# Banded attention and two MLPs on one core: an RMS norm's sums with tokens on partitions, its roots spread through device memory

## Chip, cores and metric

The kernel runs on 1 core of one Trainium2 chip. The metric is device time in microseconds (us). Before the change it is 637.46 us, the median of 3 runs (635.98 to 637.98). The engines of the core are named as in the profile: PE (TensorE), DVE (VectorE), ACT (ScalarE), POOL (GpSimd) and SP (SyncE, which here only issues transfers).

## The reference

For 2 x 768 tokens: banded attention with 8 heads of 64, then a first MLP with a squared ReLU (d_model 512, d_ff 2048), then a second, gated MLP (d_ff 1536) with an RMS norm ahead of it. The change is in that norm.

```python
x = attention(q, k, v)                       # 1536 x 512
h = np.maximum(x @ w_in, 0.0)
x = h * h @ w_out                            # first MLP
rms = np.sqrt(np.mean(x * x, axis=-1, keepdims=True) + 1e-06)
xn = x / rms * rms_g
g = xn @ w_gate
silu = g * (1.0 / (1.0 + np.exp(-g)))
out = silu * (xn @ w_val) @ w_out2           # second MLP
```

## The kernel before

The activations of both MLPs lie with the model dimension on partitions and the tokens along the free dimension: `x` and `y` are 4 blocks (e = 0..3) of 128 features. Tokens are worked in 4 chunks (c = 0..3) of 384 (`CH`). Two chunks make a half (p = 0: chunks 0 and 1; p = 1: chunks 2 and 3). Every value that goes into a product is kept as a high and a low part, and a product is three matmuls (`mm3`, lines 385 to 387). Products of a half are formed from seven block products in place of eight (`quad`), on sums and differences of the two chunks' blocks, which `norm` also prepares (lines 637, 642, 375, 376). The tiles `ar` and `x` hold the results.

The order in time around the change: attention (to about 140 us) with the first part of the first MLP between it, the rest of the first MLP, and from about 290 us its last group of hidden features, chunk by chunk (`first`), where line 517 adds the last part to `y`. When a chunk's `y` is whole, `norm_sum(c, bank)` makes its vector of 1/rms: ACT squares the four blocks (lines 602, 607), DVE adds the squares (line 608), one PE matmul with a 128x128 matrix of ones (line 610) sums over the 128 partitions and at the same time puts each token's sum on all 128 partitions, ACT takes the root on 128x384 (line 613), and DVE the reciprocal in three pieces of 128x128 (line 616). The result stands in the tile `ns` of the chunk (two tiles, c % 2). `norm(p)` then multiplies y, g and ns (line 637) and makes the operands of the gate and value products of the half. The gated MLP works over 6 pairs of hidden blocks and 2 halves; its first pair, first half, needs only chunks 0 and 1, its first pair, second half, needs chunks 2 and 3.

Weights come through SP (line 415) into two raw tiles `wraw`, and are expanded by ACT (lines 416, 418), DVE (line 420) and a split (lines 375, 376). A transfer of a weight block is issued when its raw tile is free. Queues work in order on every engine: an instruction that waits holds those behind it.

The order of all instructions is not written by hand. Each operation is added to a plan with its engine, an assumed duration, the tiles it reads and writes and, for PE, a due time; `Plan.solve` places all of them by due time, backward and forward in several rounds, takes the order with the earliest planned end, and `emit` issues the instructions in that order. Where the plan leaves PE free in two set stretches of time, it puts filler matmuls (line 1362) there. The plan takes a transfer as landed 2.6 us after its own duration (`LAT["SP"]`).

Of the kernel before, what the change touches and what calls it, by code (L numbers as in the profile page):

```python
# [12 lines left out]
F32 = mybir.dt.float32  # L13
# [6 lines left out]
P = 128  # L20
# [4 lines left out]
DM = 512  # L25
KD = DM // P
CH = 384
# [49 lines left out]
class Plan:  # L77
# [6 lines left out]
    def __init__(self):  # L84
        self.ops, self.ahead = [], set()
        self.wrote, self.read = {}, {}
# [182 lines left out]
class Mlp:  # L269
# [5 lines left out]

    def __init__(self, nc, plan, tl, main, late, psm, psl, srcs, gcol, epst, ones, ident, out):
        self.nc, self.plan, self.tl, self.out = nc, plan, tl, out
        self.gcol, self.epst, self.ones, self.ident, self.srcs = gcol, epst, ones, ident, srcs  # L280
        for k in range(KD):
            for h in "hl":
                tl.define(f"x{h}{k}", main, [P, NTOK], F32R)
        for p in range(2):
            tl.define(f"y{p}", main, [P, KD * 2 * CH], F32)
        for n in range(NM + 1):
            tl.define(f"M{n}", main if n < NM else late, [P, 1024], F32R)
        for n in range(HB):
            tl.define(f"h{n}", main, [P, 2 * CH], F32R)
        for n in range(2):  # L290
            tl.define(f"wraw{n}", main, [P, 1026], I32)
            tl.define(f"p5{n}", late, [P, CH], F32)
            tl.define(f"ns{n}", late, [P, CH], F32)
        for n in range(3):
            tl.define(f"wbits{n}", main, [P, 512], F32)
            tl.define(f"H{n}", late, [P, 512], F32R)
        for n in range(5):
            tl.define(f"ra{n}", main if n < 3 else late, [P, CH], F32)
        for n in range(4):
            tl.define(f"nq{n}", late, [P, CH], F32)  # L300
        tl.define("ar", late, [P, 24 * CH], F32R)
        for n in range(8):
            tl.define(f"b{n}", psm if n < 4 else psl, [P, 512], F32)
        self.nraw = self.nbits = self.nload = self.nact = self.nra = self.np5 = self.nnq = 0
        self.nhalf = 0
        self.clock = 0.0
        self.late = ["late"]
        self.attention_over = False
        self.w = {}
# [229 lines left out]
            self.relu2(lambda f=f: self.tl(f"b{banks[f]}")[:, :CH], [("b", banks[f])], act[f, c % 2])  # L539
        return act  # L540

    def outs(self, f0, cs, act):
        nc = self.nc
        for c in cs:
            for e in range(KD):
                bank = e % 2
                ps = lambda bank=bank: self.tl(f"b{bank}")[:, :CH]
                y, ry = (lambda e=e, c=c: self.y(e, c)), self.yres(e, c)
                for f in range(2):
                    w, rw = self.w[("out", f0 + f), e]  # L550
                    self.mm3(bank, w, act[f, c % 2][0], f == 0, f == 1, CH, rw + self.both(act[f, c % 2][1]))
                self.op("DVE", DVE(CH), lambda y=y, ps=ps: nc.vector.tensor_tensor(  # L552
                    out=y(), in0=ps(), in1=y(), op=ALU.add), [("b", bank)] + ry, ry)
                yield
# [41 lines left out]
    def norm_sum(self, c, bank):  # L596
# [3 lines left out]
        for e in range(KD):  # L600
# [5 lines left out]
            t, rt = (lambda n=n: tl(f"nq{n}")), [("nq", n)]  # L606
            self.op("ACT", ACT(CH), lambda e=e, t=t: nc.scalar.activation(t(), self.y(e, c), AF.Square), self.yres(e, c), rt)
            self.op("DVE", DVE(CH), lambda t=t: nc.vector.tensor_tensor(out=s(), in0=s(), in1=t(), op=ALU.add), rs + rt, rs, port=True)
        ps = lambda: tl(f"b{bank}")[:, :CH]
        self.op("PE", 0.75, lambda: nc.tensor.matmul(  # L610
            ps(), lhsT=self.ones, rhs=s(), start=True, stop=True, skip_group_check=True), rs, [("b", bank)],
            due=self.clock - (12.0 if bank == 7 else 0.0), mode="full", slack=NSLACK)
        self.op("ACT", ACT(CH) + 1.3, lambda: nc.scalar.activation(
            s(), ps(), AF.Sqrt, bias=self.epst, scale=1.0 / DM), [("b", bank)], rs)
        for i in range(NT):
            self.op("DVE", 0.85, lambda i=i: nc.vector.reciprocal(  # L616
                s()[:, i * P : (i + 1) * P], s()[:, i * P : (i + 1) * P]), rs, rs)

    def norm(self, p):

# [681 lines left out]
def kernel(  # L1302
# [23 lines left out]
    with ExitStack() as cx:  # L1326
        cx.enter_context(tc.manual_schedule(engines=None))
        plan, tl = Plan(), Lazy()
        main, psm = Late(tc, cx, "main"), Late(tc, cx, "psm", **space)
        late, psl = Late(tc, cx, "late"), Late(tc, cx, "psl", **space)  # L1330
        main(), psm()
        ax = ExitStack()
        ap, psa = Late(tc, ax, "attn"), Late(tc, ax, "psa", **space)
        ap(), psa()
        mlp = Mlp(nc, plan, tl, main, late, psm, psl, srcs, gcol, epst, ones, ident, out)
        fetch, count, nl, ng = scalars(nc, const, counts)
        att = Attention(nc, plan, tl, ap, psa, mlp, kq, vab, ident, nl, ng)
        plan.add("ACT", 0.45, fetch, (), ["nw"], due=0.0, lat=LAT["SP"])
# [26 lines left out]
    with tc.If(said["value"] < 1):  # L1365
        with ExitStack() as cx:
            plan, tl = Plan(), Lazy()
            main, psm = Late(tc, cx, "gmain"), Late(tc, cx, "gpsm", **space)
            main()
            late = Late(tc, cx, "glate")  # L1370
            mlp = Mlp(nc, plan, tl, main, late, psm, psm, srcs, gcol, epst, ones, ident, out)
            general_attention(tc, kq, vab, nl, ng, ident, mlp)
            for c in range(NC_ - 1):
                mlp.begin(c, None)
            mlp.rest(mlp.clock)
            plan.solve().emit()
# [62 lines left out]
```

## Time and profile before

| | |
|---|---|
| median of 3 runs | 637.46 us |
| profiled execution | 636.76 us, of which the span of instructions is 635.0 us |
| PE busy | 624.0 us (98% of the span) |
| DVE busy | 454.4 us (72%) |
| ACT busy | 421.7 us (66%) |
| POOL busy | 158.9 us (25%) |
| chain that ended last | PE 88%, DVE 4%, ACT 4%, DMA 2%, issue 1%, POOL 1% |
| PE clock granted | 0.999 of full speed |

Times of instructions are from the profiled execution and count from the first instruction of the span. A busy PE is one with a matmul in it: matmuls overlap, so one of 384 columns is listed with some 0.34 us while the next starts 0.17 us later; the spacing of the starts shows what one costs. Fill matmuls count as busy, too. "Idle before" an instruction is its engine's idle time, and the arrow says whose end it waited for.

### The profile page before, as it was taken

How to read it: one execution, taken by the hardware profiler on the slowest of the kernel's cores; microseconds unless marked ns; L12 is line 12 of the kernel's file. 1: busy time of each engine (PE TensorE's matmuls, PEld its weight loads, DVE VectorE, ACT ScalarE, POOL GpSimd, SP SyncE). 2: the span in 40 equal slices, each digit the busy share in tenths (PEclk: the TensorE clock that was granted, in tenths of full speed). 3: DMA queues.
4: the chain of work that ended last, by engine and by line, in shares of the span. 5: the costliest groups of instructions: out<-in, count | busy, mean ns of one | idle time of the engine just before them, and what ended most of it. 6: DMA issues, size and time to landing. Idle time of an engine off the chain costs nothing.

```text
span 635.0 us, 10497 instructions
## 1 busy us (share of the span) xinstructions
PE 624.0 (98%) x3740; PEld 591.7 (93%) x3740; DVE 454.4 (72%) x1007; ACT 421.7 (66%) x954; POOL 158.9 (25%) x235
## 2 busy tenths in 40 slices
PE   8899999999999999999999999999999999999996
PEld 8789899999999999999999989999999998999995
DVE  6777989859998777785569998458458458546444
ACT  5899797958977887775659877846445445453310
POOL 6442455332404300042001204221232133140000
PEclk9999999999999999999999999999999999999999
DMA  7875767101224244233000111423213114010023
GB/s 238 231 233 156 202 163 192 42 12 66 67 67 129 71 133 133 66 105 97 0 1 1 67 35 34 132 67 100 67 35 123 43 34 133 33 35 2 0 91 114
DMA packets 20845, 56.34 MB, mean 89 GB/s; under 512 B 3248, under 2 KB 6064, under 8 KB 20784
## 3 DMA queue, kind: packets, MB, share of 16 engines
q1 hardware_dynamic: 19472, 53.82, 27.9%
q10 hardware_dynamic: 1312, 1.77, 0.8%
q8 instruction: 31, 0.51, 0.3%
q14 instruction: 30, 0.25, 0.1%
HBM read 52.43 MB, written 3.15 MB: 88 GB/s over the span
## 4 chain that ended last, share of the span: by engine, by line
PE 88%; DVE 4%; ACT 4%; DMA 2%; issue 1%; POOL 1%; POOLq 0%; ACTq 0%; DVEq 0%
PE b L386 26%; PE b L385 26%; PE b L387 26%; PE tb L1065 2%; PE av L1075 2%; PE ps L1026 2%; PE b L1362 1%; DMA wraw<-in_w_in_dram 1%; ACT p L1048 1%; PE ps L1034 1%; DVE p L1044 1%; DMA wraw<-in_w_out_dram 1%; DVE ns L616 0%; DVE wbits L420 0%; DVE qs L983 0%
## 5 line engine op out<-in xcount | busy, mean ns | idle before, releaser
L385 PE MATMUL b<-xh,M 128*128 128x384 f32 x384 | 132.3, 345 | 0.2 <-ACT ra L481 0.2
L387 PE MATMUL b<-xh,M 128*128 128x384 f32 x384 | 129.1, 336 | 0.0
L386 PE MATMUL b<-xl,M 128*128 128x384 f32 x384 | 129.1, 336 | 0.0
L376 POOL TENSOR_TENSOR M<-wbits,M 128x512 fp32r<-128x512 f32 x32 | 47.2, 1480 | 158.2 <-ACT M L375 158.1
L385 PEld LDWEIGHTS b<-xh,M 128*128 128x128 f32 x384 | 72.2, 188 | 2.5 <-ACT ra L481 0.6
L386 PEld LDWEIGHTS b<-xl,M 128*128 128x128 f32 x384 | 72.1, 188 | 2.1 <-DVE xl L376 0.3
L387 PEld LDWEIGHTS b<-xh,M 128*128 128x128 f32 x384 | 72.1, 188 | 0.2
L385 PE MATMUL b<-h,M 128*128 128x384 f32 x208 | 71.7, 345 | 0.0
L386 PE MATMUL b<-h,M 128*128 128x384 f32 x208 | 70.0, 337 | 0.1
L387 PE MATMUL b<-h,M 128*128 128x384 f32 x208 | 69.7, 335 | 0.0
L742 DVE TENSOR_TENSOR y<-b,y 128x512 f32<-128x512 f32 (+1 forms) x61 | 41.6, 682 | 37.2 <-PE b L387 36.2
L375 ACT CAST M<-wbits 128x512 fp32r<-128x512 f32 x81 | 49.9, 621 | 19.5 <-PE b L387 9.9
L420 DVE SCALAR_TENSOR_TENSOR wbits<-wraw,wbits 128x512 int32<-128x512 int32 x68 | 47.3, 695 | 16.4 <-ACT wbits L418 12.6
L456 POOL TENSOR_TENSOR wbits<-wbits 128x256 f32<-128x256 f32 x16 | 13.3, 833 | 174.9 <-DVE wbits L420 174.9
L386 PE MATMUL b<-M,h 128*128 128x512 f32 (+1 forms) x146 | 56.9, 390 | 0.0
L385 PE MATMUL b<-M,h 128*128 128x512 f32 (+1 forms) x146 | 56.8, 389 | 0.0
L387 PE MATMUL b<-M,h 128*128 128x512 f32 (+1 forms) x146 | 56.8, 389 | 0.0
L1048 ACT ACTIVATE p<-p,few 128x256 f32<-128x256 f32 (+1 forms) x96 | 46.9, 497 | 12.5 <-DVE few L1044 8.7
L416 ACT ACTIVATE wbits<-wraw 128x512 f16<-128x512 bf16 x68 | 45.2, 668 | 11.9 <-POOL wbits L456 5.8
L484 DVE TENSOR_TENSOR h<-ra,h 128x384 fp32r<-128x384 f32 x64 | 39.3, 618 | 13.0 <-ACT ra L483 12.6
L552 DVE TENSOR_TENSOR y<-b,y 128x384 f32<-128x384 f32 x64 | 34.6, 551 | 13.5 <-PE b L387 13.5
L709 ACT ACTIVATE ra<-b 128x384 f32<-128x384 f32 x36 | 17.6, 491 | 39.9 <-PE b L387 39.9
(145 smaller groups left out, 1540.7 us busy)
## 6 DMA issues: line engine op xcount, KB each, us to landing
wraw<-in_w_out_dram SPq DMA_DIRECT2D x28, 512.0 KB, 3.4
wraw<-in_w_in_dram SPq DMA_DIRECT2D x16, 512.0 KB, 4.1
wraw<-in_w_gate_dram SPq DMA_DIRECT2D x12, 512.0 KB, 3.3
wraw<-in_w_val_dram SPq DMA_DIRECT2D x12, 512.0 KB, 3.3
raw<-in_kq_dram SPq DMA_DIRECT2D x16, 240.0 KB, 4.7
raw<-in_kq_dram SPq DMA_DIRECT2D x16, 208.0 KB, 4.8
v<-in_vab_dram SPq DMA_DIRECT2D x8, 384.0 KB, 3.1
v<-in_vab_dram SPq DMA_DIRECT2D x8, 256.0 KB, 3.5
```

The source lines that it names most:

```text
L375: self.op("ACT", ACT(n), lambda: nc.scalar.copy(dst()[0], src()), rs, [(x, "hi") for x in ws])
L376: self.op(eng, t(n), lambda: e.tensor_tensor(out=dst()[1], in0=src(), in1=f32(dst()[0]), op=ALU.subtract), rs + [(x, "hi") for x in ws], [ ...
L385: nc.tensor.matmul(ps, lhsT=wh, rhs=ah, start=first, stop=False, skip_group_check=True)
L386: nc.tensor.matmul(ps, lhsT=wh, rhs=al, start=False, stop=False, skip_group_check=True)
L387: nc.tensor.matmul(ps, lhsT=wl, rhs=ah, start=False, stop=last, skip_group_check=True)
L416: self.plan.add("ACT", ACT(512), lambda: nc.scalar.activation(tl(bits)[:, 256:].bitcast(F16), head(), AF.Copy), rr, rb)
L420: self.plan.add("DVE", DVE(512), lambda: nc.vector.scalar_tensor_tensor(out=bi(), in0=tail(), scalar=13, in1=bi(), op0=ALU.logical_shift_r ...
L484: self.op("DVE", DVE(CH), lambda: nc.vector.tensor_tensor(out=get()[1], in0=t(), in1=f32(get()[0]), op=ALU.subtract), rt + hi, lo, port=True)
L552: self.op("DVE", DVE(CH), lambda y=y, ps=ps: nc.vector.tensor_tensor(out=y(), in0=ps(), in1=y(), op=ALU.add), [("b", bank)] + ry, ry)
L709: self.op("ACT", ACT(CH), lambda: nc.scalar.activation(t(), src(), AF.Silu), rs, rt)
L742: self.op("DVE", DVE(a1 - a0), lambda o=o, ps=ps: nc.vector.tensor_tensor(out=o(), in0=ps(), in1=o(), op=ALU.add), [("b", bank)] + ro, ro)
L1048: self.op("ACT", 0.29 + w / 1200, lambda j=j: nc.scalar.activation(tl(f"p{m}")[:, j, :w], tl(f"p{m}")[:, j, :w], AF.Exp, bias=tl("few")[:, ...
```

## The change

The sum over the features is taken with the roles of the two matmul operands exchanged. In place of one matmul with the ones as the stationary operand and 384 tokens moving, there are three, each with 128 tokens of `ns` as the stationary operand (every third token: column i, i + 3, ...) and one column of ones moving. Their results stand in a 128x3 piece of PSUM: token 3p + i on partition p, column i. ACT's root and DVE's reciprocal work on this 128x3 (a new tile `rt`). SP then stores it to a new tile `far` in device memory, where the 384 values lie in the order of the tokens, and loads it from there to all 128 partitions of `ns`. From there on all is as before: `ns` holds 1/rms for each of the 384 tokens on every partition.

The function `outs` gets an argument `on` (empty unless given) with which ACT would carry the running `y` through PSUM. No call gives it.

```diff
-        ps = lambda: tl(f"b{bank}")[:, :CH]
-        self.op("PE", 0.75, lambda: nc.tensor.matmul(
-            ps(), lhsT=self.ones, rhs=s(), start=True, stop=True, skip_group_check=True), rs, [("b", bank)],
-            due=self.clock - (12.0 if bank == 7 else 0.0), mode="full", slack=NSLACK)
-        self.op("ACT", ACT(CH) + 1.3, lambda: nc.scalar.activation(
-            s(), ps(), AF.Sqrt, bias=self.epst, scale=1.0 / DM), [("b", bank)], rs)
-        for i in range(NT):
-            self.op("DVE", 0.85, lambda i=i: nc.vector.reciprocal(
-                s()[:, i * P : (i + 1) * P], s()[:, i * P : (i + 1) * P]), rs, rs)
+        ps, r, rr = (lambda: tl(f"b{bank}")[:, :NT]), (lambda: tl(f"rt{c % 2}")), [("rt", c % 2)]
+        far, rf = (lambda: tl(f"far{c}")), [("far", c)]
+
+        def sums():
+            for i in range(NT):
+                nc.tensor.matmul(ps()[:, i : i + 1], lhsT=s().rearrange("p (n i) -> p i n", i=NT)[:, i], rhs=self.ones[:, :1],
+                                 start=True, stop=True, skip_group_check=True)
+        self.op("PE", 0.25 * NT, sums, rs, [("b", bank)], due=self.clock - (12.0 if bank == 7 else 0.0), mode="full", slack=NSLACK)
+        self.op("ACT", ACT(NT) + 1.4, lambda: nc.scalar.activation(
+            r(), ps(), AF.Sqrt, bias=self.epst, scale=1.0 / DM), [("b", bank)], rr)
+        self.op("DVE", 0.16, lambda: nc.vector.reciprocal(r(), r()), rr, rr)
+        self.op("SP", 0.1, lambda: nc.sync.dma_start(
+            out=far().rearrange("a (p i) -> (a p) i", i=NT), in_=r()), rr, rf)
+        self.op("SP", DMA(192), lambda: nc.sync.dma_start(out=s(), in_=far().broadcast_to([P, CH])), rf, rs)
...
+            tl.define(f"rt{n}", late, [P, NT], F32)
...
+        for n in range(NC_):
+            tl.define(f"far{n}", far, [1, CH], F32)
...
+        far = Late(tc, cx, "far", space=bass.MemoryType.DRAM)
```

## Rows read from the trace of the kernel before

**Rows 1.** The page's part 1: busy time, share of the span, instructions.
```profile
PE 624.0 (98%) x3740; PEld 591.7 (93%) x3740; DVE 454.4 (72%) x1007; ACT 421.7 (66%) x954; POOL 158.9 (25%) x235
```

**Rows 2.** Table by stretches: stretch, length, busy time per engine, clock, DMA share, GB/s.
```profile
290.00:345.00 55.00, 55.00 (x315) 54.47 (x314) 36.82 (x68) 34.67 (x71) 1.61 (x1) 1.00 0.06 20
345.00:366.00 21.00, 20.92 (x118) 20.06 (x116) 19.42 (x33) 17.84 (x33) 4.53 (x5) 1.00 0.15 51
```

**Rows 3.** PE's timeline: start, duration, instruction, idle time before it and its releaser.
```profile
365.41 0.34 PE L386 MATMUL b<-xl,M 128*128 128x384 f32 x1
365.58 0.34 PE L387 MATMUL b<-xh,M 128*128 128x384 f32 x1
366.33 0.94 PE L1362 MATMUL b<-ones 128*128 128x128 f32 x6 [0.41 <-DVE ra L713]
367.02 0.43 PE L385 MATMUL b<-ar,H 128*128 128x384 f32 x1
...
376.98 0.34 PE L385 MATMUL b<-xh,M 128*128 128x384 f32 x1
```

**Rows 4.** PE's groups of instructions from 345 to 372 us: count, busy us, mean ns.
```profile
L1362 PE MATMUL b<-ones 128*128 128x128 f32 x10 | 1.7, 284 | 0.4 <-DVE ra L713 0.4
```

**Rows 5.** Chain of waits that ended last: start, us, engine, tile, line, count.
```profile
33.05 1.24 PE av L1075 x20
...
348.48 0.65 PE b L610 x2
```

**Rows 6.** DVE's timeline, columns as in Rows 3.
```profile
355.61 0.94 DVE L616 RECIPROCAL ns<-ns 128x128 f32<-128x128 f32 x1
356.47 0.49 DVE L608 TENSOR_TENSOR ns<-ns,nq 128x384 f32<-128x384 f32 x1
...
363.72 0.94 DVE L616 RECIPROCAL ns<-ns 128x128 f32<-128x128 f32 x1
365.12 0.69 DVE L420 SCALAR_TENSOR_TENSOR wbits<-wraw,wbits 128x512 int32<-128x512 int32 x1 [0.45 <-issue]
365.72 0.55 DVE L713 TENSOR_TENSOR ra<-b,ra 128x384 f32<-128x384 f32 x1
...
366.66 0.61 DVE L637 SCALAR_TENSOR_TENSOR nq<-y,gcol,ns 128x384 f32<-128x384 f32 x1
```

**Rows 7.** ACT's timeline, columns as in Rows 3.
```profile
359.23 1.28 ACT L613 ACT_TABLE_LOAD   x1
360.52 0.58 ACT L613 ACTIVATE ns<-b,epst 128x384 f32<-128x384 f32 x1
...
364.39 0.63 ACT L418 ACTIVATE wbits<-wbits 128x512 int32<-128x512 int16 x1
```

**Rows 8.** Tile ns: duration ns least/median/most, first and last start, shapes.
```profile
L616 DVE RECIPROCAL ns<-ns x12: 893/941/952, 309.1 to 363.7; 128x128 f32<-128x128 f32 x12
L610 PEld LDWEIGHTS b<-ns,ones x8: 187/188/188, 305.8 to 358.3; 128*128 128x128 f32 x8
```

**Rows 9.** Small instructions of other lines (1055 and 1146), columns as in Rows 8.
```profile
L1055 DVE RECIPROCAL few<-few x48: 151/164/167, 10.8 to 133.0; 128x2 f32<-128x2 f32 x48
...
L1146 ACT ACTIVATE warm<-epst x1: 204/204/204, 3.7 to 3.7; 128x1 f32<-128x1 f32 x1
```

**Rows 10.** DMA issues: tile, queue, count, KB each, us from issue to landing.
```profile
v<-in_vab_dram SPq DMA_DIRECT2D x8, 64.0 KB, 3.6
out_dram<-y SPq DMA_DIRECT2D x6, 256.0 KB, 2.0
...
gcol<-in_rms_g_dram SPq DMA_DIRECT2D x1, 2.0 KB, 4.7
```

**Rows 11.** SP's timeline from 290 to 385 us: start and duration of the issue.
```profile
348.69 0.33 SPq L415 DMA_DIRECT2D wraw<-in_w_gate_dram  x1
358.73 0.33 SPq L415 DMA_DIRECT2D wraw<-in_w_val_dram  x1
365.83 0.33 SPq L415 DMA_DIRECT2D wraw<-in_w_out_dram  x1
```

More of the change, by code (lines that the diff above doesn't have):

```diff
@@ L269, with __init__ @@
 class Mlp:
-    def __init__(self, nc, plan, tl, main, late, psm, psl, srcs, gcol, epst, ones, ident, out):
+    def __init__(self, nc, plan, tl, main, late, far, psm, psl, srcs, gcol, epst, ones, ident, out):
         self.nc, self.plan, self.tl, self.out = nc, plan, tl, out
@@ L540, in plain, with outs @@
         return act
-    def outs(self, f0, cs, act):
+    def outs(self, f0, cs, act, on=()):
         nc = self.nc
@@ L548, in outs @@
                 y, ry = (lambda e=e, c=c: self.y(e, c)), self.yres(e, c)
+                if e in on:
+                    self.op("ACT", ACT(CH), lambda y=y, ps=ps: nc.scalar.copy(ps(), y()), ry, [("b", bank)])
                 for f in range(2):
                     w, rw = self.w[("out", f0 + f), e]
-                    self.mm3(bank, w, act[f, c % 2][0], f == 0, f == 1, CH, rw + self.both(act[f, c % 2][1]))
+                    self.mm3(bank, w, act[f, c % 2][0], f == 0 and e not in on, f == 1, CH, rw + self.both(act[f, c % 2][1]))
+                if e in on:
+                    self.op("ACT", ACT(CH), lambda y=y, ps=ps: nc.scalar.copy(y(), ps()), [("b", bank)], ry)
+                    yield
+                    continue
                 self.op("DVE", DVE(CH), lambda y=y, ps=ps: nc.vector.tensor_tensor(
@@ L1334 @@
         ap(), psa()
-        mlp = Mlp(nc, plan, tl, main, late, psm, psl, srcs, gcol, epst, ones, ident, out)
+        mlp = Mlp(nc, plan, tl, main, late, far, psm, psl, srcs, gcol, epst, ones, ident, out)
         fetch, count, nl, ng = scalars(nc, const, counts)
@@ L1370 @@
             late = Late(tc, cx, "glate")
-            mlp = Mlp(nc, plan, tl, main, late, psm, psm, srcs, gcol, epst, ones, ident, out)
+            far = Late(tc, cx, "gfar", space=bass.MemoryType.DRAM)
+            mlp = Mlp(nc, plan, tl, main, late, far, psm, psm, srcs, gcol, epst, ones, ident, out)
             general_attention(tc, kq, vab, nl, ng, ident, mlp)
```

## The prediction

> **What bounds the kernel now.** I read the busy shares first: TensorE (PE) works for 624.0 of 635.0 us [rows 1]. A change on another engine is therefore worth only what it gives back of the PE's remaining time, or what it adds by stopping it. The change touches the stretch from 290 to 385 us, so the table by stretches came next. From 290 to 345 us PE is busy 55.00 of 55.00 us, DVE only 36.82; from 345 to 366 us PE has 20.92 of 21.00, but DVE 19.42 and ACT 17.84 [rows 2]. The norms of chunks 0 and 1 lie in the first stretch, beside a PE that waits for nobody; those of chunks 2 and 3 lie where DVE and ACT are nearly full.
>
> Then PE's own timeline, since a busy PE can hide filler. Two kinds of loss stand in it.
>
> The sums themselves: in the chain of waits the two records of chunk 2's matmul with ones stand with 0.65 us [rows 5], so the four norm sums cost PE 2.6 us.
>
> The stall: product matmuls start 0.17 us apart (365.41, 365.58), but behind the one at 365.58 the next PE instruction starts at 366.33, 0.75 us later, and it is filler (L1362) that computes nothing the output needs. Three fills (six matmuls) last from 366.33 to 367.02, 0.23 us each; there are five (ten matmuls) from 345 to 372. So at most 0.58 + 5 x 0.23 = 1.73 us is lost here. The idle time ahead of the filler ends with DVE's L713 [rows 3, 4].
>
> Why L713 is late needs two timelines. On DVE the last reciprocal of chunk 3 runs from 363.72 to 364.66, then DVE stands idle 0.45 us, then L420 (365.12), then L713 (365.72) [rows 6]. On ACT the L418 that L420 needs starts at 364.39 and ends at 365.02; before it stand a table load of 1.28 us (359.23), the root (360.52, 0.58) and what follows [rows 7]. So both engines are late at once: the reciprocals hold DVE until 364.66, ACT holds it 0.45 us longer.
>
> **The change, part by part.**
>
> *Reciprocals.* Out go 12 of 941 ns, median [rows 8]; in come 4 on 128x3. The nearest row is a reciprocal on 128x2: 164 ns [rows 9]. DVE gains 12 x 0.94 - 4 x 0.16 = 10.6 us, half of it (5.3 us) for chunks 2 and 3, in the stretch where DVE is full. On PE that is worth nothing by itself; it is worth the stall as far as DVE causes it.
>
> *Roots.* ACT's root on 128x384 takes 0.58 us [rows 7]; an activation on 128x1 took 0.204 us [rows 9]. ACT gains some 0.38 us per norm. The table loads stay: between 0 and no gain, I count none. The 0.38 us together with an earlier start can pull L418 forward by about as much as DVE stood idle for it.
>
> *Matmuls.* Two matmuls of 384 columns (fp32 is recorded as two) become three products, so six records, each with its own 128x128 weight load and one column moving. No row shows this. Below: 20 small ones with weights of 64 columns (av) take 1.24 us, 0.062 each, so 6 x 0.062 = 0.37 us [rows 5]. Above: the record of a 128x128 load is 188 ns [rows 8]; if nothing overlaps, and the stride of three words costs nothing more, 6 x 0.188 = 1.13 us. The nearest are the fills: 128x128 fp32 weights, 0.69 us for six [rows 3]. I take 0.69 against 0.65, +0.04 each, so +0.2 us for four, with ends at 4 x (0.37 - 0.65) = -1.1 and 4 x (1.13 - 0.65) = +1.9 us.
>
> *The two transfers.* After the reciprocal SP stores 1.5 KB to device memory, waits for it to land, and issues a load of it to all 128 partitions (192 KB). Stores of 256 KB land 2.0 us after issue; the load of g, made of 4-byte pieces like the new 12-byte ones, took 4.7; loads of 64 KB took 3.6 [rows 10]. For the store I take 2.0 (same direction, same queue), with 4.7 as the upper end; for the load 3.6, with 4.7 above and the store's 2.0 below.
>
> The Trainium skill (DMA: Bandwidth & Descriptors, Anatomy of one DMA) gives about 2.0 us of fixed cost plus bytes over 436 GB/s, measured on another issuing path; for 192 KB that is an estimate of 2.45 us. The row of 64 KB disagrees: 3.6 us. By the page the pair would take 4.5 us and the vector would come 1.1 us earlier than below.
>
> *The vector's date.* For chunk 3 today: root starts at 360.52, the vector is whole at 364.66, 4.1 us [rows 6, 7]. After: 0.20 + 0.16 + 2.0 + 3.6, plus three hand-overs that I put at 0.1 each, 6.3 us. The start moves the other way: the third sum (L608, 356.47) had to wait until chunk 2's reciprocal of 355.61 was over (0.94 us); without it that sum runs 0.86 us earlier [rows 6]. So the vector lands at about 360.52 - 0.86 + 6.3 = 366.0 instead of 364.66. Its first reader, L637, ran at 366.66 today because DVE had other work first [rows 6]. That work, with 5.3 us taken off DVE, is the cover: the reader is not late, and the work before it (L713 among it) moves forward. What is late next after L713 is ACT's L418.
>
> For chunks 0 and 1 the vector comes some 2 us later than now. The cover is PE's chunk-3 work, which needs no norm, and DVE's 18 idle us of 55 [rows 2]. I count nothing; without that cover each late us before gate products of the first half is one us of PE.
>
> *SP's queue.* A wait there holds every transfer behind it: first for the reciprocal, then for the landing of the store. Weight loads are issued at 348.69, 358.73 and 365.83 [rows 11]. Chunk 2's pair would be issued from about 350 to 352.5 and chunk 3's from 360 to 362.5, both between these. I count nothing. A load that falls behind a pair is up to 2.5 us late; the converter behind it then starts late, and only a load that ACT waits for costs PE.
>
> *outs.* Its new argument is empty in every call; it emits what it did. DRAM space and the unused general path issue nothing.
>
> *The plan.* Every engine's order comes from one list of due times and durations solved for the whole kernel. New durations here may reorder instructions elsewhere, even in the attention stage. No row bounds this; for size, the stall of 1.73 us is what one such order costs today. I take 0 for the likeliest and +-2 us for the range.
>
> **Sum.** The stall is 1.73 us at most; since ACT's 0.45 us holds part of it, I take 1.5 back. -1.5 + 0.2 = -1.3 us against the profiled execution's 636.76 gives 635.5. That execution is 0.70 us under the runs' median of 637.46, so on the median: 636.1 us.
>
> **Rivals.**
>
> *A, the stall stays, the time with it.* ACT, not DVE, is the last to come in 364 to 365 us, and its two table loads (1.28 us each) stay. For it: DVE's idle 0.45 us right before L420 [rows 6]. Against: ACT also gets 0.38 us and an earlier start. Then only +0.2 is left: 637.7.
>
> *B, slower: the vector of chunk 3 becomes the bound.* The second half's first gate product starts at 376.98, right behind a product of the output [rows 3]; the eight L637 and what hangs on them must pass DVE between the vector's landing and it or the products behind it. At the upper ends the path is 0.36 + 4.7 + 4.7 + 0.3 = 10.1 us and lands at 369.8, 3.1 us after the 366.66 at which the first reader runs today. It decides from 366.66 on: each us of landing beyond it is one of PE, less what the emptied DVE catches up (at most the 1.5 us that the stall would have given back). So +3.1 + 0.2 without and +1.6 + 0.2 with it: 639.3 to 640.8. For it: small pieces, and g's 4.7 us [rows 10]. Against: the stores' 2.0. A rule of the Trainium skill speaks for it: pieces under 512 B are written by read-modify-write (DMA: Bandwidth & Descriptors, Specifications); no row here shows a store of such pieces.
>
> *C, the new order decides.* The plan changes elsewhere, 1 to 3 us either way: 634 to 639, about even in sign. For it: one solution for all engines; against: the durations outside the norm are unchanged.
>
> *D, the small matmuls are dear* (1.13 each): -1.5 + 1.9 = +0.4, 637.9, not distinguishable from A by time, but by the trace.
>
> **Chances.** 0.3% is 1.9 us, about what a measurement here can tell from no change. Forecast 0.45, A 0.17, D 0.05, B 0.13, C 0.20. Faster (below 635.5): a bit under half of the forecast's own spread (0.21), half of C (0.10), and 0.03 of the rest: 0.34. Slower (above 639.4, or with the spread of B and C above it): 0.10 of B, 0.08 of C, 0.02 of the rest: 0.20. Same: 0.46. The likeliest case's own range is 634.5 to 637.7. With B's and C's ends the range is 633.4 to 639.6.
>
> **What would show it.** Right: no reciprocal above 0.3 us on DVE; the fills between 345 and 372 gone or down to one or two; about 0.7 us of PE per norm sum; the second half's gate products start 1 to 2 us earlier than 376.98. Wrong: PE or DVE waits for a transfer into ns; a weight load issued late behind a pair and a converter waiting for it; more fill than now; or a difference that arises before 290 us, where the kernel's text is the same.

## The result, and the profile after

The changed kernel takes 645.24 us (median of 5 runs, 644.04 to 645.64), the one before 637.46 (5 runs, 635.98 to 638.10): ratio 1.0116, 95% interval 1.0100 to 1.0132. It is 7.8 us slower, where 636.1 was forecast and 639.6 was the upper end. The profiled execution of after took 644.04 us, with a span of 642.2, 7.2 more than before's 635.0.

Lines have moved: L610 is now L623 (sums), L613 L626 (root), L616 L628 (reciprocal), L637 L651 (first reader of `ns`), L713 L727, L385 to L387 are L388 to L390, L1362 is L1377 (fill), L415 and L420 are L418 and L423. L629 is the store, L631 the load.

Busy shares and the first group of products (part 1 and one line of part 5; against [rows 1]):

```profile
PE 628.1 (98%) x3754; PEld 596.0 (93%) x3754; DVE 444.9 (69%) x999; ACT 420.3 (65%) x954; POOL 160.4 (25%) x235
...
L388 PE MATMUL b<-xh,M 128*128 128x384 f32 x384 | 131.9, 343 | 2.6 <-DVE ra L727 2.3
```

DVE's busy time fell by 9.5 us and its instructions by eight (12 reciprocals less, 4 more), as they should; PE is busy 4.1 us longer. A busy share can't say why, but the group has 2.3 us of idle time that ended with DVE's L727. The table by stretches says where, with before's last stretch behind it (columns as in [rows 2]):

```profile
290.00:345.00 55.00, 54.66 (x316) 54.34 (x315) 30.27 (x60) 31.63 (x66) 2.45 (x1) 1.00 0.13 27
345.00:366.00 21.00, 20.69 (x118) 20.16 (x118) 14.62 (x30) 17.88 (x36) 4.53 (x5) 1.00 0.21 60
366.00:380.00 14.00, 10.99 (x45) 9.56 (x45) 9.92 (x21) 5.93 (x12) 0.00 (x0) 0.76 0.22 53
```

```profile
366.00:380.00 14.00, 13.65 (x68) 11.67 (x69) 13.96 (x30) 10.05 (x21) 0.00 (x0) 1.00 0.12 39
```

The first norm sum starts at 305.70 us here and at 305.93 before, so nothing is lost ahead of it. From 290 to 366 PE loses 0.6 us more than before. From 366 to 380 it is busy 10.99 of 14 us instead of 13.65, and the granted clock is 0.76 of full speed instead of 1.00. In [rows 2] DVE was busy 19.42 of 21 us from 345 to 366; now it is 14.62. The work that the change took away has become waiting. PE's timeline of that place (columns as in [rows 3]):

```profile
367.57 0.34 PE L389 MATMUL b<-ar,M 128*128 128x384 f32 x1
367.76 0.34 PE L390 MATMUL b<-ar,M 128*128 128x384 f32 x1
370.43 0.69 PE L388 MATMUL b<-xh,M 128*128 128x384 f32 x1 [2.33 <-DVE ra L727]
370.92 0.52 PE L389 MATMUL b<-xl,M 128*128 128x384 f32 x1
371.24 0.52 PE L390 MATMUL b<-xh,M 128*128 128x384 f32 x1
372.43 1.65 PE L1377 MATMUL b<-ones 128*128 128x128 f32 x6 [0.67 <-DVE ra L727]
```

PE stands 2.33 us for L727, later 0.67 us for the next L727, the fill included (it is written to the bank that L727 reads, so it waits as well). From 370.43 on products start 0.32 us apart (370.92, 371.24) where they started 0.19 apart before the wait (367.57, 367.76) and 0.17 in [rows 3]. DVE's timeline and SP's say what L727 waited for:

```profile
358.91 0.62 DVE L651 SCALAR_TENSOR_TENSOR nq<-y,gcol,ns 128x384 f32<-128x384 f32 x1 [2.23 <-DMA ns<-far]
...
362.39 0.18 DVE L628 RECIPROCAL rt<-rt 128x3 f32<-128x3 f32 x1 [0.38 <-ACT rt L626]
364.55 0.57 DVE L692 TENSOR_TENSOR b<-b,p 128x384 f32<-128x384 f32 x1 [1.98 <-PE b L390]
...
368.76 1.15 DVE L651 SCALAR_TENSOR_TENSOR nq<-y,gcol,ns 128x384 f32<-128x384 f32 x2 [3.65 <-DMA ns<-far]
369.82 0.55 DVE L727 TENSOR_TENSOR ra<-b,ra 128x384 f32<-128x384 f32 x1
```

```profile
360.15 0.33 SPq L418 DMA_DIRECT2D wraw<-in_w_val_dram  x1
362.59 0.32 SPq L629 DMA_DIRECT2D far<-rt  x1
364.48 0.32 SPq L631 DMA_DIRECT2D ns<-far  x1
...
371.47 0.33 SPq L418 DMA_DIRECT2D wraw<-in_w_out_dram  x1
```

The product that L727 reads ended at 368.10 (367.76 + 0.34). But L727 stands behind two L651 in DVE's queue, and L651 waited 3.65 us for chunk 3's load, issued at 364.48. L423 stands behind them too, so the raw tile comes free late, and the next weight load is issued at 371.47 instead of 365.83 [rows 11]. The 364.55 line is not the cause: it waited for a product, and L651 was next in line behind it.

ACT's timeline shows that chunk 2's vector was late as well, and what that did:

```profile
359.56 0.51 ACT L378 CAST xh<-nq 128x384 fp32r<-128x384 f32 x1 [1.11 <-DVE nq L651]
...
360.80 1.28 ACT L626 ACT_TABLE_LOAD   x1
362.09 0.26 ACT L626 ACTIVATE rt<-b,epst 128x3 f32<-128x3 f32 x1
```

L651 at 358.91 waited 2.23 us for chunk 2's load; the cast of its result (L378, 359.56) waited for it, and chunk 3's table load and root stand behind that cast. In [rows 7] the table load started at 359.23; here at 360.80. One late vector made the next one late.

The chain of waits, back from the end, goes through the same instructions (columns as in [rows 5]):

```profile
348.81 0.87 PE b L623 x6
...
364.48 4.26 DMA ns<-far
368.76 0.72 DVE nq L651 x2
369.82 0.55 DVE ra L727
```

The sums' six records stand with 0.87 us instead of 0.65 [rows 5], but the product behind them is slower, too. PE's timelines, after's first, show what a sum costs with both:

```profile
305.70 1.04 PE L623 MATMUL b<-ones,ns 128*128 128x1 f32 x6
...
307.04 0.34 PE L390 MATMUL b<-xh,M 128*128 128x384 f32 x1
```

```profile
305.93 0.81 PE L610 MATMUL b<-ns,ones 128*128 128x384 f32 x2
...
306.91 0.34 PE L387 MATMUL b<-xh,M 128*128 128x384 f32 x1
```

Two products stand between the lines each time. So a sum costs PE 1.34 - 0.99 = 0.35 us more than before. The tiles `ns` and `rt`, and the DMA issues (columns as in [rows 8] and [rows 10]):

```profile
L623 PEld LDWEIGHTS b<-ones,ns x24: 251/260/263, 305.5 to 358.1; 128*128 128x128 f32 x24
```

```profile
L626 ACT ACTIVATE rt<-b,epst x4: 247/263/265, 308.2 to 362.1; 128x3 f32<-128x3 f32 x4
L628 DVE RECIPROCAL rt<-rt x4: 166/176/177, 308.5 to 362.4; 128x3 f32<-128x3 f32 x4
```

```profile
ns<-far SPq DMA_DIRECT2D x4, 192.0 KB, 4.3
...
far<-rt SPq DMA_DIRECT2D x4, 1.5 KB, 2.0
```

The store cost what was taken, 2.0 us; the load 4.3 instead of 3.6; the root 0.26 instead of 0.20, the reciprocal 0.18 instead of 0.16. The small sums load their weights in 260 ns, where the weights of ones, contiguous, took 188 [rows 8].

Why does the reader stand ahead of L727? In the plan, an operation is ready for a reader on another engine `LAT` after its end, but for one on its own engine only `SAME` after it, and `SAME["SP"]` is 0. Store and load are both SP's. So the load was planned 0.1 us after the store's start, with no time for the store to land, and the vector 3.4 us after the store's start (0.1 + 0.72 + 2.6). With the reciprocal's 0.16 and DVE's `LAT` of 0.28 that is 3.9 us after the reciprocal's start. On the chip it came 6.35 us after it (362.39 to 368.74). So the order is made for a vector about 2.5 us earlier than the real one.

Where the time goes can be counted on PE's two timelines from start to start: a product of 384 columns takes 0.17 us, one of 512 columns 0.23, and what goes beyond that is lost. From the first norm sum to the end, after takes 336.5 us and before 329.1, 7.4 more:

- The four sums, each with the slower product behind it: 4 x 0.35 = 1.4 us.
- Waits ahead of 366 us that before doesn't have: 1.5 us. The two large ones, 0.5 us each, are at 342.11 (for DVE's L487) and 361.41 (for L702). Both stand in DVE's queue behind an L651 that waited for a load (2.74 us for chunk 1's, 2.23 us for chunk 2's) and the work held up with it.
- From 366 to 380 us: 7.2 us lost, against 2.3 for the whole of before's stall, so 4.9. The 7.2 are two waits for L727 (2.50 and 0.87 us), four pairs of fill matmuls (4 x 0.23 at full speed), and 2.9 us more because the instructions from 370.4 to 377 us run at a granted clock of 0.50.

That makes 7.8. The last matmul stands 0.4 us nearer the end than in before, which leaves the 7.4. Each number is from one execution.

### The profile page after: what moved, and what is told of

The parts are those of the page before. It is cut to its first block, busy times and chain, and to the rows that moved or that the text cites. A ratio compares the mean times of both kernels' runs of the same rounds, so it can differ in the third digit from the quotient of the medians.

```text
span 642.2 us, 10536 instructions
## 1 busy us (share of the span) xinstructions
PE 628.1 (98%) x3754; PEld 596.0 (93%) x3754; DVE 444.9 (69%) x999; ACT 420.3 (65%) x954; POOL 160.4 (25%) x235
## 4 chain that ended last, share of the span: by engine, by line
PE 77%; DVE 9%; ACT 7%; DMA 4%; issue 1%; POOL 1%; DVEq 0%; ACTq 0%; POOLq 0%; SPq 0%
PE b L389 24%; PE b L388 23%; PE b L390 23%; ACT p L1062 2%; DMA ns<-far 2%; PE tb L1079 1%; PE b L1377 1%; PE av L1089 1%; DMA wraw<-in_w_in_dram 1%; PE ps L1040 1%; PE ps L1048 1%; DVE p L1058 1%; ACT h L485 1%; ACT pt L1081 1%; ACT ra L486 1%
## 5 line engine op out<-in xcount | busy, mean ns | idle before, releaser
L388 PE MATMUL b<-xh,M 128*128 128x384 f32 x384 | 131.9, 343 | 2.6 <-DVE ra L727 2.3
L390 PE MATMUL b<-xh,M 128*128 128x384 f32 x384 | 129.2, 337 | 0.0
L379 POOL TENSOR_TENSOR M<-wbits,M 128x512 fp32r<-128x512 f32 x32 | 48.1, 1508 | 165.2 <-ACT M L378 164.8
L388 PEld LDWEIGHTS b<-xh,M 128*128 128x128 f32 x384 | 72.2, 188 | 4.8 <-DVE ra L727 2.7
L390 PEld LDWEIGHTS b<-xh,M 128*128 128x128 f32 x384 | 72.2, 188 | 0.2
L388 PE MATMUL b<-h,M 128*128 128x384 f32 x208 | 71.7, 345 | 0.0
L390 PE MATMUL b<-h,M 128*128 128x384 f32 x208 | 69.7, 335 | 0.0
L378 ACT CAST M<-wbits 128x512 fp32r<-128x512 f32 x81 | 50.0, 620 | 20.5 <-PE b L390 9.8
L423 DVE SCALAR_TENSOR_TENSOR wbits<-wraw,wbits 128x512 int32<-128x512 int32 x68 | 47.2, 694 | 14.7 <-ACT wbits L421 11.2
L459 POOL TENSOR_TENSOR wbits<-wbits 128x256 f32<-128x256 f32 x16 | 13.3, 830 | 175.8 <-DVE wbits L423 175.8
L388 PE MATMUL b<-M,h 128*128 128x512 f32 (+1 forms) x146 | 56.9, 390 | 0.0
L390 PE MATMUL b<-M,h 128*128 128x512 f32 (+1 forms) x146 | 56.8, 389 | 0.0
L419 ACT ACTIVATE wbits<-wraw 128x512 f16<-128x512 bf16 x68 | 45.1, 666 | 12.3 <-POOL wbits L459 5.2
L487 DVE TENSOR_TENSOR h<-ra,h 128x384 fp32r<-128x384 f32 x64 | 39.2, 616 | 15.6 <-ACT ra L486 15.2
L421 ACT ACTIVATE wbits<-wbits 128x512 int32<-128x512 int16 x68 | 42.7, 631 | 1.1
```

Of the source, the lines that this page charges most:

```text
L378: self.op("ACT", ACT(n), lambda: nc.scalar.copy(dst()[0], src()), rs, [(x, "hi") for x in ws])
L379: self.op(eng, t(n), lambda: e.tensor_tensor(out=dst()[1], in0=src(), in1=f32(dst()[0]), op=ALU.subtract), rs + [(x, "hi") for x in ws], [ ...
L388: nc.tensor.matmul(ps, lhsT=wh, rhs=ah, start=first, stop=False, skip_group_check=True)
L390: nc.tensor.matmul(ps, lhsT=wl, rhs=ah, start=False, stop=last, skip_group_check=True)
L419: self.plan.add("ACT", ACT(512), lambda: nc.scalar.activation(tl(bits)[:, 256:].bitcast(F16), head(), AF.Copy), rr, rb)
L421: self.plan.add("ACT", ACT(512), lambda: nc.scalar.activation(bi(), tl(bits)[:, 256:].bitcast(I16), AF.Copy, scale=65536.0), rb, rb)
```

## Experiments

Whether an experiment's order differs from the other kernels' matters below. Instruction by instruction up to the first norm, before, after and experiments 2, 4, 6, 7, 8, 11 and 12 have one order (family A); experiments 1, 3, 5, 9 and 10 come from another round of the plan's solution and have a second order (family B; experiment 5 leaves it some 25 us ahead of the first norm).

### 1. The plan told what the transfers take

```diff
-        self.op("PE", 0.25 * NT, sums, ...
+        self.op("PE", 0.3 * NT, sums, ...
-        self.op("SP", 0.1, lambda: nc.sync.dma_start(           # store
+        self.op("SP", 2.1, lambda: nc.sync.dma_start(
-        self.op("SP", DMA(192), ..., rf, rs)                    # load
+        self.op("SP", DMA(192), ..., rf, rs, lat=3.7)
```

> The changed kernel with other durations in the plan alone: the store of the 128x3 occupies SP for 2.1 us (in the changed kernel the plan lets the load start 0.1 us after the store, since both are on SP; the trace shows 1.9 to 2.3 us), the load lands 4.4 us after its issue (trace: 4.3), three matmuls take 0.9. Theory 'order': the loss comes from an order built on a vector that is expected 3.4 us after the reciprocal and comes after 6.2; DVE stands before L651 and L727 behind it is late. Then 637.5 to 639.5 us, no PE idle above 0.7 us between 345 and 380, clock 1.00 there. Rival 'path': two transfers make the path from the last sum to the second half's products too long in any order: 642 to 646 us. Rival 'sums': the loss lies in the matmuls and elsewhere: 644 to 646.

Measured: 637.64 us, ratio to before 0.9999 (0.9985 to 1.0013). The same instructions (but for six fills more) and the same transfers, in another order, and 7.6 us are gone. It is the low end of what theory 'order' expected, and below both rivals. DVE's timeline and PE's fill, family B:

```profile
367.76 0.55 DVE L727 TENSOR_TENSOR ra<-b,ra 128x384 f32<-128x384 f32 x1
...
368.69 0.61 DVE L651 SCALAR_TENSOR_TENSOR nq<-y,gcol,ns 128x384 f32<-128x384 f32 x1
```

```profile
368.37 1.16 PE L1377 MATMUL b<-ones 128*128 128x128 f32 x8
```

L651 comes after the L727 that held PE, and no longer waits; the granted clock stays at 1.00 from 366 to 380. Some stall is left, 0.91 us of fill between 368.37 and 369.28; counted from start to start, PE loses 2.3 us here between 345 and 380, as much as in before. The chain there goes POOL L459, ACT L419, ACT L378, DVE L379, DVE L423, DVE L727: the expansion of a weight block, not the norm.

### 2. The old norm for chunk 3 alone

```diff
+        if c == 3:
+            ...   # the old matmul with ones, root on 128x384, three reciprocals
+            return
```

> The changed kernel, but chunk 3's norm as before (one matmul with ones, root and reciprocals of 128x384, no transfers). Theory 'order' and rival 'path': what costs is chunk 3's vector; 637.5 to 639.5 us (three dearer matmuls of +0.25 us each and about 0.5 us at 342 us stay). Rival 'sums': 643 to 645 us.

Measured: 640.06 us, 1.0027 (1.0014 to 1.0040). Giving chunk 3 its old norm back, without transfers, returns 5.2 of the 7.8 us. The number is 0.6 us above the upper end expected. Its profiled execution came to the first norm sum at 308.07 us, 2.1 later than before's, in the same order; from there to the end it took 330.8 us, before 329.1 and after 336.5. What moved the attention by 2 us I can't say (experiment 8 shows it, too).

### 3. The new norm for chunk 3 alone

```diff
+        if c < 3:
+            ...   # the old matmul with ones, root on 128x384, three reciprocals
+            return
```

> Chunk 3's norm alone as in the changed kernel, chunks 0 to 2 as before. Theory 'order' and 'path': most of the loss is back, 642 to 645.5 us, with a PE stall of 2 to 3.5 us near 368 us behind an L651 that waits for the load. Rival 'sums' (loss spread over four norms): 639 to 640 us.

Measured: 639.82 us, 1.0032 (1.0018 to 1.0045): inside what rival 'sums' expected, and 2.2 us below what 'order' and 'path' expected. The order is of family B, so it isn't a clean half of the change. L662 (here the reader) waited 2.68 us for the load all the same, at 369.70, but two L738 (L727 of after) stood ahead of it, and only the third waited: PE lost 1.79 us at 371.31 instead of 2.33 and 0.67, and the clock of that stretch is 1.00. The price of a late vector hangs on what stands behind its reader.

### 4. No transfers

```diff
-        self.op("DVE", 0.16, lambda: nc.vector.reciprocal(r(), r()), rr, rr)
-        self.op("SP", ...   # store and load
+        self.op("DVE", 0.16, lambda: nc.vector.reciprocal(r(), r()), rr, rr + rs)
```

> The changed kernel without the two transfers: the readers take ns as it stands (sums of squares), so the output is not the norm's; matmuls, roots and reciprocals of 128x3 stay. Theory 'order' and 'path': 636.5 to 638.5 us, no stall near 368. Rival 'sums': 641 us or more.

Measured: 637.44 us, 0.9996 (0.9980 to 1.0011), family A. The kernel leaves out store and load, and its readers take the sums of squares as they stand. So this is the change with transfers that are free and land at once, and it is no faster than before. One fill of 0.83 us remains between 345 and 377 us:

```profile
373.04 0.83 PE L1374 MATMUL b<-ones 128*128 128x128 f32 x6
```

Counted from start to start, PE loses 1.1 us here between 345 and 380, and 2.3 in before. So 1.2 us of the stall come back, and the sums take them: 4 x 0.35 = 1.4. From 366 to 380 us DVE is busy 14.00 of 14.00 us here. Freed from its reciprocals, DVE is full there all the same.

### 5. The store's landing told, nothing else

```diff
-        self.op("SP", 0.1, lambda: nc.sync.dma_start(           # store
+        self.op("SP", 2.1, lambda: nc.sync.dma_start(
```

> The changed kernel with one number of the plan changed: the store of the 128x3 occupies SP for 2.1 us in the plan instead of 0.1, so that the plan lets the load start when the store has landed. The load's landing (plan 3.3 us, trace 4.3) and all else stay. Theory 'store': the missing wait of 2 us is what spoils the order: 637 to 640 us. Rival 'load': the 1.0 us that the load lands late weighs as much: 641 to 643.5. Rival 'matmuls' (0.9 against 0.75 in the plan): above 643.5.

Measured: 638.01 us, 1.0003 (0.9984 to 1.0023). One number of the plan, the landing of the store, does what the three of experiment 1 did. It is family B, so the family's own share is still in it: experiments 10 and 12 take that apart.

### 6. Contiguous tokens per matmul

```diff
-                ... lhsT=s().rearrange("p (n i) -> p i n", i=NT)[:, i], ...
+                ... lhsT=s()[:, i * P : (i + 1) * P], ...
-            out=far().rearrange("a (p i) -> (a p) i", i=NT), in_=r()), rr, rf)
+            out=far().rearrange("a (i p) -> (a p) i", i=NT), in_=r()), rr, rf)
```

> The changed kernel with 128 neighbouring tokens as stationary operand in place of every third; the 128x3 then goes to memory in pieces of 4 bytes in place of 12. The plan and so the order of instructions is that of the changed kernel. If the stride of three is what makes a weight load take 260 ns: 188 ns again, six records in 0.66 to 0.69 us, 4 x 0.2 = 0.8 us less, 644.2 to 644.8. If it is not: 0.87 again. If smaller pieces store later (up to the 4.7 us of g): the vector comes up to 2.5 us later and the time is 646 to 648; if not, the store lands after 2.0 again.

Measured: 671.81 us, 1.0522 (1.0490 to 1.0553), 24 us above the upper end expected. The weight loads fell to 192 ns as hoped, and the six records of a sum from 0.90 to 0.58 us (start of the first to start of the next product). But the store now consists of 384 pieces of 4 bytes instead of 128 of 12:

```profile
ns<-far SPq DMA_DIRECT2D x4, 192.0 KB, 4.7
...
far<-rt SPq DMA_DIRECT2D x4, 1.5 KB, 8.5
```

```profile
382.62 8.48 DMA far<-rt
391.15 4.65 DMA ns<-far
```

8.5 us instead of 2.0 in the middle of four (8.1 to 11.3), for the same 1.5 KB. PE now waits long behind the earlier vectors, too (8.20 us at 382.07, behind chunk 2's). Behind chunk 3's load PE stands 7.91 us for L727, where after's stood 2.33: 5.6 us more for 6.5 us more of landing, in the same order. That is nearly the slope of rival B.

### 7. The stall filled

```diff
+        AT = min(o.start for o in plan.ops if o.eng == "PE" and o.start > 362.2)
+            [(AT, lambda: nc.tensor.matmul(tl("b0")[:, CH:], lhsT=ones, rhs=ones, ...))] * 10
```

> The changed kernel, same order, with 10 filler matmul calls (0.23 us each) on PE ahead of the product that starts at 370.43 in its trace, into PSUM bank 0, which nobody uses then (the plan's own fillers write bank 3, which L727 reads). They compute nothing the output needs. Theory 'clock': of the loss some 3.3 us are the 6.6 us at half clock behind the idle stretch; with PE kept at work the clock stays at 1.00 between 370 and 377 and the time is 641.5 to 643.5 us. Rival 'stall alone': the low clock is paid anyway or costs nothing: 644.5 to 646.

Measured: 642.64 us, 1.0069 (1.0045 to 1.0092), 2.6 us under after. The ten calls do nothing for the output; they keep PE at work while it waits, in after's order (L728 is L727 here). PE's timeline and the stretch:

```profile
368.73 2.39 PE L1381 MATMUL b<-ones 128*128 128x128 f32 x20
371.36 0.44 PE L389 MATMUL b<-xh,M 128*128 128x384 f32 x1 [0.23 <-DVE ra L728]
371.64 0.33 PE L390 MATMUL b<-xl,M 128*128 128x384 f32 x1
371.81 0.34 PE L391 MATMUL b<-xh,M 128*128 128x384 f32 x1
```

```profile
366.00:380.00 14.00, 12.56 (x75) 11.32 (x74) 10.31 (x22) 7.84 (x16) 0.00 (x0) 1.00 0.24 54
```

Products behind the wait again start 0.17 us apart (371.64, 371.81), at a clock of 1.00, 2.4 GHz, where after's showed 0.32 and 0.76. So 2.6 of the 7.8 us (1.9 by the profiled executions, 336.5 against 334.6 us from the first norm sum to the end) were not the wait itself but the speed after it, the lower level of 1.2 GHz; 0.76 is the mean of both levels over the stretch. It is less than the 2.9 us counted above, since a faster PE comes sooner to the second wait for L727 (1.21 us idle here, 0.67 in after).

### 8. A load that does not wait for the store

```diff
-        self.op("SP", DMA(192), lambda: nc.sync.dma_start(out=s(), in_=far().broadcast_to([P, CH])), rf, rs)
+        self.op("SP", DMA(192), lambda: nc.sync.dma_start(out=s(), in_=self.rows), rf, rs)
+            mlp.rows = kq[1, 1][:, :CH]
```

> The changed kernel, same order, but the load of the vector reads 128 rows of 1.5 KB of an input instead of the stored vector, and so isn't held until the store has landed (the output is not the norm's). Theory 'late vector in that order': the vector comes some 2 us earlier, as the plan thought, no DVE wait of more than 1.5 us before L651 and L727, clock 1.00: 638 to 640.5 us. Rival 'bad order': the order is dear even with the vector in time: 642 to 645. Beside it: if reading the same 1.5 KB for all 128 partitions is what makes the load take 4.3 us, distinct rows land sooner (3.3 to 3.6); if not, 4.3 again.

Measured: 641.04 us, 1.0034 (1.0017 to 1.0052), 0.5 us above the upper end expected and below the rival's range. The kernel leaves the stored roots unused: its readers take rows of an input. The load is issued at 363.49, 0.4 us behind the store, so the 2 us are gone from the queue; but side by side both land later:

```profile
ns<-in_kq_dram SPq DMA_DIRECT2D x4, 192.0 KB, 5.2
...
far<-rt SPq DMA_DIRECT2D x4, 1.5 KB, 3.8
```

```profile
368.03 1.15 DVE L651 SCALAR_TENSOR_TENSOR nq<-y,gcol,ns 128x384 f32<-128x384 f32 x2 [1.91 <-DMA ns<-in_kq_dram]
```

The reader's wait falls from 3.65 to 1.91 us, and the clock stays at 1.00. The order is still after's, with two L651 ahead of L727; from the first norm sum to the end it takes 331.5 us, 4.9 less than after. So it is the order and the late vector together that cost. Whether 128 different rows by themselves land sooner than one row read 128 times isn't shown, since here a store is under way beside them.

### 9. Contiguous weights, and the order of the tokens undone by the reader

```diff
+                ... lhsT=s()[:, i * P : (i + 1) * P], ...        # the 12-byte store stays; the plan as in 1
+                    out=tmp[n]().rearrange("p (i n) -> p i n", i=NT), in0=self.y(e, c).rearrange("p (i n) -> p i n", i=NT),
+                    scalar=self.gcol[:, e : e + 1], in1=tl(f"ns{c % 2}").rearrange("p (n i) -> p i n", i=NT),
```

> A version made of what the runs showed: the plan told the two transfers' times (2.1 and 4.4 us), 128 neighbouring tokens as stationary operand (weight loads of 188 instead of 260 ns), the 128x3 stored in pieces of 12 bytes as in the changed kernel, and L651 reads the vector with a stride of three words. Theory: four norm sums cost what they did before the change (0.6 to 0.69 us each instead of 0.87), the stride costs DVE nothing, and no PE stall above 1.5 us: 636 to 637.5 us, at or just under the kernel before. Rival: a strided read makes L651 dearer than 0.61 us (16 of them): 638 to 640.

Measured: 638.88 us, 1.0022 (1.0012 to 1.0033), inside the rival's range and slower than experiment 1 by 1.2 us. Tile `ns` (columns as in [rows 8]):

```profile
L623 PEld LDWEIGHTS b<-ones,ns x24: 186/192/192, 303.8 to 356.4; 128*128 128x128 f32 x24
...
L651 DVE SCALAR_TENSOR_TENSOR nq<-y,gcol,ns x16: 728/740/841, 316.5 to 380.9; 128x384 f32<-128x384 f32 x16
```

The weight loads gain 68 ns each, 24 of them, and a sum with the product behind it costs 0.03 us more than before's instead of 0.35, as the theory had it; the sixteen L651 take 0.13 us each more than the 0.61 of experiment 1, 2.1 us of DVE in all, where experiment 1 had it busy 13.37 of 14 us from 366 to 380. That this is the 1.2 us is argued, not shown.

### 10. The kernel before with other numbers in its plan

```diff
-        self.op("PE", 0.75, ...                 # the sum
+        self.op("PE", 0.65, ...
-        self.op("ACT", ACT(CH) + 1.3, ...       # the root
+        self.op("ACT", ACT(CH) + 1.4, ...
-            self.op("DVE", 0.85, ...            # the reciprocals
+            self.op("DVE", 0.87, ...
```

> The kernel before, instruction for instruction the same work, with three durations of the plan set to what its trace shows (norm matmul 0.65 for 0.75, reciprocal 0.87 for 0.85, root with table load 0.1 more). It shows how far another solution of the plan moves the time by itself. Theory: the plan falls into another order from the first instructions on, and the time moves by less than 1.5 us: 636 to 639. Rival: orders differ by as much as the change costs: below 634 or above 641.

Measured: 636.22 us, 0.9981 (0.9970 to 0.9993). Eight fills apart, not one instruction differs from before; the order is family B's. It is the fastest kernel of this study, ahead of before and after.

### 11. The store in three transfers of one column

```diff
-        self.op("SP", 0.1, lambda: nc.sync.dma_start(
-            out=far().rearrange("a (p i) -> (a p) i", i=NT), in_=r()), rr, rf)
+        self.op("SP", 0.1, lambda: [nc.sync.dma_start(
+            out=far().rearrange("a (p i) -> (a p) i", i=NT)[:, i : i + 1], in_=r()[:, i : i + 1]) for i in range(NT)], rr, rf)
```

> The changed kernel, same order, with the 128x3 stored by three transfers of one column each (128 pieces of 4 bytes) in place of one (128 pieces of 12 bytes). It tells why 384 pieces of 4 bytes landed after 8.5 us. If it is the number of pieces in one transfer: each of the three lands in 2 to 3 us, the load starts 2.5 to 4 us after the first store, and the time is 646 to 652. If it is the size of a piece: each takes 7 us or more, 665 us or more.

Measured: 662.76 us, one run, between the two ranges. The first of a chunk's three stores lands 1.8 to 2.0 us after its issue, the second 4.0 to 4.9, the third 6.2 to 7.6; the load is issued 7.1 to 8.5 us after the first. So 128 pieces of 4 bytes can land in 1.8 us, as fast as 128 of 12, and the next ones to the same 1.5 KB, issued less than 1 us later, each land 2.5 to 3.3 us behind the one before. Whether the number of pieces or the neighbouring bytes make experiment 6's 8.5 us stays open.

### 12. Experiment 5 in family A's order

```diff
+                n += 1
+                if n < 11 and (best is None or end < best[0] - 1.0e-6) or n == 11:    # the round before and after come from
+        self.op("SP", 2.1, lambda: nc.sync.dma_start(                                 # store, was 0.1
```

> The plan told the store's 2.1 us as in e5, and held to that round of its solution from which the kernels before and after come: all instructions up to the first norm sum (306 us) then stand in the order of those two, and only the rest is ordered anew. e5 also changed the order from the start, which e10 showed to be worth 1.2 us by itself. Theory 'store': 638 to 640 us, the first norm sum at 306 us as in both, and from it to the end 329.5 to 331.5 us (329.1 before, 336.5 in the changed kernel). Rival: what e5 gave back came from its early order: 642 us or more, 333 us or more from the first norm sum on.

Measured: 639.71 us, 1.0032 (1.0018 to 1.0046). All up to the first norm stands as before and after have it, and only the order around the norm is new. DVE (L728 is L727, L652 is L651):

```profile
365.24 0.69 DVE L424 SCALAR_TENSOR_TENSOR wbits<-wraw,wbits 128x512 int32<-128x512 int32 x1 [1.38 <-ACT wbits L422]
365.84 0.55 DVE L728 TENSOR_TENSOR ra<-b,ra 128x384 f32<-128x384 f32 x1
...
367.45 0.55 DVE L728 TENSOR_TENSOR ra<-b,ra 128x384 f32<-128x384 f32 x1
...
368.64 0.62 DVE L652 SCALAR_TENSOR_TENSOR nq<-y,gcol,ns 128x384 f32<-128x384 f32 x1 [0.17 <-DMA ns<-far]
```

The two L728 go first, L652 waits 0.17 us, and the clock is 1.00 from 366 to 380 us:

```profile
366.00:380.00 14.00, 13.30 (x65) 10.77 (x64) 13.21 (x28) 8.58 (x18) 0.00 (x0) 1.00 0.21 51
```

The first norm sum starts at 305.76, and from it to the end it takes 330.8 us, both as theory 'store' expected. That is 5.5 of the 7.8 us, with the early order held, for one number of the plan. That number moves many instructions behind the norm; that the place of the L651 is what counts among them is read from the timelines. The idle 1.38 us ahead of L424 waits for ACT's L422: the weight block again.

## Why the prediction was wrong

**The bound and the stall** were read rightly: PE, with DVE and ACT both late at 365. What I drew from it was too much. Counted from start to start the stall is 2.3 us (1.73 by the prediction's count, which leaves out the slower product behind each fill). Without transfers 1.2 of it come back (experiment 4); with them, even in a better order, next to nothing: experiments 1 and 12 lose 2.3 and 2.1 us in the same place, behind ACT's expansion of weights. Rival A was nearer the truth on this term.

**Reciprocals, roots.** The terms were right (DVE's busy time fell by 9.5 us, 10.6 were forecast), and were worth nothing beyond those 1.2, which only a kernel without the transfers got.

**Matmuls.** +0.04 each were taken, 0.35 measured, so 1.4 instead of 0.2 us in all. It lay between the ends given (up to +1.9). The fills, to which I held it, have contiguous weights of 188 ns, and the new ones load in 260. With contiguous weights it was +0.03 (experiment 9), and the +0.04 would have been right: what was put at nothing is the stride of three words.

**The two transfers.** 2.0 was right, 4.3 for 3.6 was low, and in all the vector comes 6.65 us after the root's start instead of 6.3. That error is 0.35 us and not the cause. The Trainium skill (DMA: Bandwidth & Descriptors, Specifications) gives 512 B as the least piece for line rate, with a read-modify-write below; pieces of 12 bytes, 128 of them, cost no more here than the 2.0 us of [rows 10], pieces of 4, 384 of them, cost 8.5. That rule of the Trainium skill spoke for rival B; the row of this store does not bear it out at 12 bytes.

**The vector's date** is the step that failed: "That work, with 5.3 us taken off DVE, is the cover: the reader is not late, and the work before it (L713 among it) moves forward." Three things were wrong in it. The root was to start 0.86 us earlier and started 1.57 later (362.09 against 360.52 [rows 7]). The sum did move as forecast (357.46 us against 358.33), but the root stood in ACT's queue behind the cast that waited 1.11 us for chunk 2's vector, and behind the two instructions that follow the cast. The vector landed at 368.74 instead of 366.0. And the work ahead of the reader was no longer ahead of it: with shorter durations and a load that the plan believed to be done early, the plan put two L651 in front of L727. I had read in `LAT` that the plan grants a transfer 2.6 us of landing, and not that a reader on the same queue is granted none. Experiments 5 and 12 turn on the planned landing of the store alone, and with it 5.5 of the 7.8 us go in the early order of before and after (experiment 12).

**SP's queue.** Counted at nothing, and rightly in itself: the weight loads at 350.31 and 360.15 left before each pair. The late one (371.47) is a consequence of DVE's wait.

**The clock** had no term. A wait of 2.33 us at that place cost 1.9 to 2.6 us more behind it (experiment 7).

**Rival B** had the mechanism, a reader of `ns` that waits, and the right sign; it put the price on the landing beyond 366.66 and got +1.8 to +3.3. Landing was 2.1 us beyond it. Missing were the clock's 1.9 to 2.6 us, 1.2 of the sums, and the order of the queue, which let the wait reach products that don't use `ns` at all. The upper end of the range, 639.6, doesn't follow from the rivals either: B's own end was 640.8. **Rival C**, another order elsewhere, 1 to 3 us either way: up to the norm nothing changed its place here. Experiment 10 sizes it: 1.2 us for the same instructions, fills apart (637.46 against 636.22).

**What the change costs when it is ordered well**, like compared with like:

| | old norm | new norm, landing told |
|---|---|---|
| family A | 637.46 (before) | 639.71 (experiment 12) |
| family B | 636.22 (experiment 10) | 638.01 (5), 637.64 (1) |

So 1.4 to 2.3 us slower in either. From the first norm sum to the end, in one profiled execution each, it is 330.8 against 329.1 us in A and 330.5 against 328.5 in B: 1.7 to 2.0, of which the sums are 1.4. In A, experiment 4 has the new sums and no transfers, and 637.44: there sums and stall cancel, and 2.27 us come with the transfers. Of these 1.6 lie behind the first norm sum (330.8 against 329.2); 1.0 of them is the stall that isn't won back. The other 0.7 differ between executions ahead of the norm, where the profiles are up to 2 us apart in one and the same order; why stays open.

## What to carry to other kernels

Before counting a freed engine as a gain, ask which instruction will wait in its queue, and what stands behind it: an in-order queue turns a late operand of a later stage into a stall of the present one. Where a planner makes the order, read what it believes of each new pair of operations, above all of two transfers on one queue, where the second needs the first's landing. And compare a change with the old code under the same order, since another order of the same instructions alone was worth 1.2 us here.

## What the hardware showed that was not expected

- A store of 1.5 KB landed in 2.0 us as 128 pieces of 12 bytes, in 8.5 us (8.1 to 11.3) as 384 pieces of 4 bytes (experiment 6).
- A load of 192 KB, one row of 1.5 KB to 128 partitions, takes 4.3 us; one of 512 KB of weights 3.3 to 3.5 in the same execution (gate and val blocks). Distinct rows took 5.2 beside a store (experiment 8).
- Loading 128x128 fp32 weights with a step of three words is recorded with 260 ns, contiguous with 192 (experiment 6), and the one-column matmuls on them start 0.17 us apart, contiguous 0.11. The Trainium skill (TensorE: Matmul & The Clock Gate, LDWEIGHTS) lets the time go by the number of columns, which is the same in both; the measurement differs.
- DVE reading one fp32 operand with a step of three words takes 0.74 us for 128x384 instead of 0.61 (experiment 9, where its other operands go in three blocks of 128).
- After 2.33 us without a matmul PE ran at half pace from 370.43 to about 377, at a granted clock of 0.50, the level of 1.2 GHz; with small matmuls in the gap it did not (experiment 7).
